# Windowed attention and a mixture of attention experts on one core: keys on partitions, a mask factor, and row-tile units in place of per-head stages

## The chip, the cores and the metric

One core of a Trainium2 chip runs the kernel. The metric is the device time of one execution in microseconds. TensorE multiplies, VectorE and ScalarE work on its results in PSUM and on SBUF, GpSimd makes masks and casts, and DMAs move data between memory and SBUF, issued here by SyncE or by ScalarE.

## The reference

Two attention layers stand one behind the other. The first has 4 batches, 8 heads, 768 positions and 64 columns per head. A query sees the 96 keys up to and with its own and the 8 first keys; a bias falls with the distance, with a slope per head. The second takes the result (8 x 64 = 512 columns) into four attention experts of one head each, causal, and adds up the two that a router picks.

```python
scores = scale * np.matmul(q, k.transpose(0, 1, 3, 2))
is_global = pos[None, :] < int(n_global)
is_local = (rel >= 0) & (rel < int(n_local))
dist = np.where(is_global & ~is_local, float(n_local), np.abs(rel).astype(np.float32))
scores = scores + (-slopes[:, None, None] * dist[None, :, :])[None, :, :, :]
scores = np.where(is_global | is_local, scores, -1000000000.0)
a = np.exp(scores - np.max(scores, axis=-1, keepdims=True))
x = (a / (np.sum(a, axis=-1, keepdims=True) + 1e-09)) @ v    # heads side by side: B, S, 512
for e in range(E):
    a = softmax(causal(scale * (x @ wq[e]) @ (x @ wk[e]).T))
    out += weight[e] * (a @ (x @ wv[e]) @ wo[e])             # weight: softmax over the two best logits, else 0
```

Inputs q, k and v are random numbers of size 0.1, the weights of size 0.05.

## The kernel before

It works in two stages, and a scheduler orders the instructions on each engine. The attention stage loops over batch and head. Per head q, k and v are loaded with rows on partitions (`qL`, `kL`, `VL`, lines 114 to 117), q and k are transposed in fp32 on TensorE, six pieces each (lines 123 and 127), and copied to f16 by VectorE. Then, for each of six row tiles of 128 queries, up to three key tiles are visited: the first, the one before and the diagonal one. Each visit is a chain of small steps, with queries on partitions: the score `sc` (line 139, TensorE, 64 rows of the array), distance times slope added (`L`, line 142, VectorE), exponential with its row sum (line 148, ScalarE), a transpose of the probabilities (`at`, line 155, TensorE, 128 rows), its copy (line 157, VectorE), and the product with v (`zp`, line 158). At the end of a row tile the result is divided by the row sum, transposed in fp32 (line 165) and copied (line 166); a head's result goes to a DRAM tensor, `xT_bridge`.

The expert stage loops over four batches. It loads the bridge, makes router weights for each row tile (lines 193 to 218), and for each expert loads and casts the weights again and projects q and k (lines 242 and 248, 512 and 256 columns) and v (line 257). Then, for each row tile and expert, it makes all causal scores in one row (line 277), copies them to SBUF (line 279), masks the diagonal on GpSimd (line 280), takes the row maximum (line 285) and the exponential (line 289), transposes and copies each 128 columns of probabilities (lines 294 and 297), multiplies with the values (line 298), scales, transposes (line 307) and applies the output matrix (line 310).

All DMAs are issued by SyncE. PSUM pools with one to three buffers set how far one step may run ahead of the next.

Of the kernel before, what the change touches and what calls it, by code (L numbers as in the profile page):

```python
# [14 lines left out]
Iden = mybir.ActivationFunctionType.Identity  # L15

HUGE = 1.0e30
MAXN = 512
# [3 lines left out]
def kernel(  # L22
# [8 lines left out]
    P = 128  # L31
    mm = nc.tensor.matmul
    dma = nc.default_dma_engine.dma_start

    B, H, S, Dh = q.shape
    assert S % P == 0
    n_rt = S // P
    Bm, Sm, Dm = out.shape
    E = moe_w_gate.shape[1]
    Hd = moe_wq.shape[2]  # L40
    assert Dm == H * Dh
    nko = Dm // P
# [307 lines left out]
```

## Time and profile before

| what | us |
|---|---|
| median of 3 runs | 897.18 |
| lowest and highest | 896.14, 905.7 |
| profiled execution: span from first to last instruction | 896.5 |

The profiled execution is told by its span alone; the median of the runs is 0.7 us longer. The page gives, per engine, how much of the span it was busy; PE is TensorE's matmuls, PEld its weight loads, which overlap with them, DVE VectorE, ACT ScalarE, POOL GpSimd. A matmul's duration in the trace includes the time until its last result is in PSUM, so the distance between two starts tells more of the engine's rate than the duration does.

### The profile page before, as it was taken

What the parts mean: (1) busy time and instruction counts of PE and PEld (TensorE: products, weight loads), DVE (VectorE), ACT (ScalarE), POOL (GpSimd) and SP (SyncE); (2) the same over time, 40 slices, a digit from 0 to 9 for tenths busy, and PEclk for the clock granted to TensorE, in tenths of its full rate; (3) what the DMA queues carried; (4) which work ended last, traced back from release to release, by engine and by line L of the source; (5) the groups of instructions that cost most, each with busy time, mean ns of one, the idle gap of its engine ahead of it and who ended that gap; (6) DMA issues with size and microseconds to landing.
All of it is one profiled execution on the core that took longest, in us unless ns stands there. A gap on an engine that the chain in (4) does not pass through costs nothing.

```text
span 896.5 us, 14769 instructions
## 1 busy us (share of the span) xinstructions
PE 745.3 (83%) x3744; PEld 337.4 (38%) x3744; DVE 736.6 (82%) x3890; ACT 299.0 (33%) x1276; POOL 31.1 (3%) x114
## 2 busy tenths in 40 slices
PE   6888898888888888889888588788778887888876
PEld 3444444444444444444444242234223432334222
DVE  6888888888888888888888468878788878877886
ACT  4343434343443434343433222232222322232221
POOL 1000000000000000000000001000100010000100
PEclk9999999999999999999999995557555675558555
DMA  8212121121212121212110431003200220010000
GB/s 158 63 32 63 32 57 37 45 49 45 50 34 60 32 63 31 63 32 61 33 27 6 105 83 42 24 23 79 65 24 29 61 53 24 13 42 7 24 24 23
DMA packets 110820, 40.79 MB, mean 46 GB/s; under 512 B 102544, under 2 KB 106640, under 8 KB 110736
## 3 DMA queue, kind: packets, MB, share of 16 engines
q1 hardware_dynamic: 110736, 39.87, 17.9%
q8 instruction: 29, 0.48, 0.2%
q14 instruction: 55, 0.45, 0.2%
HBM read 30.42 MB, written 9.44 MB: 44 GB/s over the span
## 4 chain that ended last, share of the span: by engine, by line
PE 59%; DVE 25%; issue 7%; ACT 5%; DMA 2%; SPq 0%; POOL 0%; ACTq 0%; POOLq 0%
PE sc L139 9%; PE at L155 9%; PE ztp L165 6%; PE tp L123 5%; PE tp L127 5%; PE pqk L277 4%; PE atp L294 4%; PE zp L158 4%; PE o_ps L310 3%; ACT A L148 3%; PE pqk L248 3%; DVE rmax L285 3%; PE pqk L242 3%; DVE L L279 3%; PE zp L298 2%
## 5 line engine op out<-in xcount | busy, mean ns | idle before, releaser
L148 ACT ACTIVATE A<-L 128x128 f16<-128x128 f32 x480 | 145.8, 304 | 267.0 <-DVE L L142 209.6
L155 PE MATMUL at<-ident,A 128*128 128x128 f16 x480 | 135.5, 293 | 13.3 <-ACT A L148 8.1
L289 ACT ACTIVATE A<-L,nrm 128x128 f16<-128x128 f32 (+5 forms) x96 | 63.8, 665 | 188.0 <-DVE nrm L287 166.5
L139 PE MATMUL sc<-kT,qT 64*128 64x128 f16 x480 | 117.8, 274 | 0.0
L158 PE MATMUL zp<-Vt,at_sb 128*128 128x64 f16 x480 | 101.6, 250 | 13.2 <-DVE at_sb L157 11.7
L157 DVE COPY at_sb<-at 128x128 f16<-128x128 f16 x480 | 104.5, 219 | 8.9 <-PE at L155 5.4
L165 PE MATMUL ztp<-ident,z_sb 128*64 128x128 f32 x192 | 81.0, 422 | 29.8 <-DVE z_sb L163 26.9
L148 ACT ACTIVATION_READ_ACCUMULATOR A<-L 128x1 f32 x480 | 89.5, 186 | 0.0
L297 DVE COPY at_sb<-atp 128x128 f16<-128x128 f16 x336 | 64.5, 220 | 28.9 <-PE atp L294 23.5
L123 PE MATMUL tp<-ident,qL 128*64 128x128 f32 x192 | 80.7, 421 | 8.8 <-DMA qL<-in_q_dram 3.7
L294 PE MATMUL atp<-ident,A 128*128 128x128 f16 x336 | 76.5, 291 | 13.3 <-ACT A L289 12.6
L127 PE MATMUL tp<-ident,kL 128*64 128x128 f32 x192 | 80.7, 421 | 2.5 <-DVE qT L124 1.6
L155 PEld LDWEIGHTS <-A 128*128 128x128 f16 x480 | 50.9, 107 | 83.5 <-ACT A L148 72.5
L142 DVE SCALAR_TENSOR_TENSOR L<-ld,sc 128x128 f32<-128x128 f32 x288 | 80.0, 278 | 0.0
L298 PE MATMUL zp<-V,at_sb 128*128 128x64 f16 x336 | 64.8, 239 | 13.4 <-DVE at_sb L297 12.1
L166 DVE CAST zt_all<-ztp 64x128 f16<-64x128 f32 x192 | 54.2, 282 | 26.3 <-PE ztp L165 14.7
L158 PEld LDWEIGHTS <-at_sb 128*128 128x128 f16 x480 | 59.0, 126 | 39.0 <-DVE at_sb L157 28.0
L163 DVE TENSOR_SCALAR z_sb<-zp,rs_inv 128x64 f32<-128x64 f32 x192 | 54.0, 281 | 21.1 <-PE zp L158 14.2
L277 PE MATMUL pqk<-kT,qT 64*128 64x512 f16 (+3 forms) x128 | 55.8, 443 | 10.3 <-DVE L L279 7.6
L279 DVE COPY L<-pqk 128x512 f32<-128x512 f32 (+3 forms) x128 | 63.2, 497 | 0.5
L310 PE MATMUL o_ps<-wo,zt_sb 64*128 64x512 f16 x96 | 57.9, 603 | 6.3 <-DVE nrm L287 3.0
L298 PEld LDWEIGHTS <-at_sb 128*128 128x128 f16 x336 | 31.5, 109 | 75.0 <-DVE at_sb L297 30.2
(72 smaller groups left out, 1000.9 us busy)
## 6 DMA issues: line engine op xcount, KB each, us to landing
qL<-in_q_dram SPq DMA_DIRECT2D x32, 192.0 KB, 2.8
kL<-in_k_dram SPq DMA_DIRECT2D x32, 192.0 KB, 2.9
VL<-in_v_dram SPq DMA_DIRECT2D x32, 192.0 KB, 2.5
out_dram<-o_sb SPq DMA_DIRECT2D x24, 256.0 KB, 2.0
xT_bridge<-zt_all SPq DMA_DIRECT2D x32, 96.0 KB, 2.2
xt<-xT_bridge SPq DMA_DIRECT2D x16, 192.0 KB, 3.5
wqe<-in_moe_wq_dram SPq DMA_DIRECT2D x16, 128.0 KB, 2.3
wke<-in_moe_wk_dram SPq DMA_DIRECT2D x16, 128.0 KB, 2.3
```

Of the source, the lines that this page charges most:

```text
L123: nc.tensor.transpose(tps[:Dh, :], qL[:, ct, :], ident32[:, :])
L127: nc.tensor.transpose(tps[:Dh, :], kL[:, ct, :], ident32[:, :])
L139: mm(sc[:, :], lhsT=qT[:Dh, ri * P:(ri + 1) * P], rhs=kT[:Dh, ci * P:(ci + 1) * P], start=True, stop=True)
L148: nc.scalar.activation(asl, L[:, :], func=Exp, accum_out=acc[:, :])
L155: nc.tensor.transpose(at_ps[:, :], asl, ident[:, :])
L157: nc.vector.tensor_copy(at_sb[:, :], at_ps[:, :])
L158: mm(z_psum[:, :], lhsT=at_sb[:, :], rhs=Vt[:, ci, :], start=(idx == 0), stop=(idx == ncol - 1))
L165: nc.tensor.transpose(zt_ps[:Dh, :], z_sb[:, :Dh], ident32[:, :])
L277: mm(sc[:, :csz], lhsT=qTe[:Hd, ri * P:(ri + 1) * P], rhs=kTe[:Hd, c0:c0 + csz], start=True, stop=True)
L279: nc.vector.tensor_copy(L[:, c0:c0 + csz], sc[:, :csz])
L294: nc.tensor.transpose(at_ps[:, :], A[:, ci * P:(ci + 1) * P], ident[:, :])
L298: mm(z_psum[:, :], lhsT=at_sb[:, :], rhs=Vte[:, ci, :], start=(ci == 0), stop=(ci == ri))
```

## The change

The kernel is written anew. Work is cut into 24 units: one unit is 128 rows of one batch with all eight heads and all four experts. Scores are made with keys on partitions, so that the exponentials are already what the product with v needs as its stationary operand; nothing is transposed between. No maximum is subtracted. The mask and the distance bias are a factor on the exponentials, `M` (for a row tile's own keys, 128 columns, and for those of the tile before, 96 columns, with zeros up to 128 in `A1`) or `M0` for the first tile. The eight first keys of all heads are handled as one 64-row product (`KG`, `ag`, `VG`), with the bias put into `VG`. A column of ones beside v gives the row sums.

Loads bring q, k and v of all heads for a unit's 128 rows, GpSimd casts them to f16, and the weights are loaded once at the start, by DMAs that ScalarE issues. The result of the attention layer, `x16`, stays on chip and is transposed for the projections. q and k of an expert batch grow row tile by row tile in `QK2`, the values in `V2`. Score matmuls use 64 rows of the array, at partitions 0 to 63 and 64 to 127 in turn (`par`).

The order is written by hand: iteration i works on the attention of unit i, the projections and expert scores of unit i-1 and the expert values and output of unit i-2, and each engine keeps the order of the code. At the end the row sums are checked, and `general_path` computes everything again, in the manner of the kernel before, where one lies outside 0.05 to 60,000.

In the diff, the lines of the kernel before that go are not repeated: all of its two stages go.

```diff
+    def load(u):
+        b, ri = divmod(u, n_rt)
+        rows = slice(ri * P, (ri + 1) * P)
+        qk32 = ring3.tile([P, 2, H, Dh], F32, name="qk32")
+        v32 = ring3.tile([P, H, Dh], F32, name="v32")
+        nc.sync.dma_start(qk32[:, 0, :, :], q[b, :, rows, :].rearrange("h s d -> s h d"))
+        nc.sync.dma_start(qk32[:, 1, :, :], k[b, :, rows, :].rearrange("h s d -> s h d"))
+        nc.sync.dma_start(v32[:, :, :], v[b, :, rows, :].rearrange("h s d -> s h d"))
+        raw[u] = (qk32, v32)
...
+    w32 = const.tile([P, 4, nko, E, Hd], F32, name="w32")
+    for n, w in enumerate((moe_wq, moe_wk, moe_wv)):
+        for e in range(E):
+            nc.scalar.dma_start(w32[:, n, :, e, :], w[e].rearrange("(ko kp) d -> kp ko d", kp=P))
...
+    for b in range(B):
+        for h in range(H):
+            nc.scalar.dma_start(vg32[h * N_G:(h + 1) * N_G, b, :], v[b, h, 0:N_G, :])
...
+    M = const.tile([P, 2, 2, 2, P + N_L], FH, name="M")
+    M0 = const.tile([P, 2, 2, 2, P], FH, name="M0")
+    for h in range(H):
+        hf, pr, par = h // 4, (h // 2) % 2, h % 2
+        act.activation(M0[:, hf, par, pr, :], d0[:, :], func=Exp, scale=-slopes[h])
+    for h in range(H):
+        hf, pr, par = h // 4, (h // 2) % 2, h % 2
+        act.activation(M[:, hf, par, pr, :], d[:, :], func=Exp, scale=-slopes[h])
...
+    act.activation(bm[:, :], bm[:, :], func=Exp)
...
+    def make_vg(b):
+        pool.tensor_tensor(
+            VG[0:NL, b, :, 0:Dh], vg32[:, b, :].unsqueeze(1).to_broadcast([NL, H, Dh]),
+            bm[0:NL, :].unsqueeze(2).to_broadcast([NL, H, Dh]), op=Alu.mult)
+        pool.tensor_copy(VG[0:NL, b, :, Dh:DV], bm[0:NL, :].unsqueeze(2))
...
+    def cast(u):
+        qk32, v32 = raw.pop(u)
+        qk16 = ring2.tile([P, 2, H, Dh], FH, name="qk16")
+        pool.tensor_copy(qk16[:, :, :, :], qk32[:, :, :, :])
+        pool.tensor_copy(V1[u % NV][:, :, 0:Dh], v32[:, :, :])
+        T[u, "qk16"] = qk16
+    def transposes(u):
+        b, ri = divmod(u, n_rt)
+        qk16 = T.pop((u, "qk16"))
+        ps = wtile([P, 2, H // 2, P], FH, "tq")
...
+                nc.tensor.transpose(ps[:, s, p, :], qk16[:, s, 2 * p:2 * p + 2, :], ident[:, :])
+        qkT = ring3.tile([P, 2, H // 2, P], FH, name="qkT")
+        dve.tensor_copy(qkT[:, :, :, :], ps[:, :, :, :])
+        T[u, "qkT"] = qkT
+        if ri == 0:
+            kg = KG[b % 2]
+            for par in range(2):
+                L = slice(par * Dh, (par + 1) * Dh)
+                for p in range(H // 2):
+                    c = (2 * p + par) * N_G
+                    pool.tensor_copy(kg[L, p, c:c + N_G], qkT[L, 1, p, 0:N_G])
...
+    def scores1(u, hf):
+        b, ri = divmod(u, n_rt)
+        qkT = T[u, "qkT"]
+        sc = psS.tile([P, 2, 2, 2 * P], F32, name="sc", tag="s")
+        for pr in range(2):
+            p = 2 * hf + pr
+            for prev in range(2 if ri else 1):
+                for par in range(2):
+                    L = slice(par * Dh, (par + 1) * Dh)
+                    kt = T[u - 1, "qkT"] if prev else qkT
+                    o = sc[:, par, pr, P:P + N_L] if prev else sc[:, par, pr, 0:P]
+                    mm(o, lhsT=kt[L, 1, p, :], rhs=qkT[L, 0, p, 0:N_L] if prev else qkT[L, 0, p, :],
+                       start=True, stop=True)
+        A = A1[(2 * u + hf) % NA]
+        w = P + N_L if ri else P
+        act.activation(A[:, :, :, 0:w], sc[:, :, :, 0:w], func=Exp, scale=scale1)
+        m = M[:, hf, :, :, :] if ri else M0[:, hf, :, :, :]
+        dve.tensor_tensor(A[:, :, :, 0:w], A[:, :, :, 0:w], m, op=Alu.mult)
+        T[u, "A", hf] = A
...
+        qkT = T[u, "qkT"]
+        ps = wtile([P, P], F32, "sg")
+        for p in range(H // 2):
+            mm(ps[:, :], lhsT=KG[b % 2][:, p, :], rhs=qkT[:, 0, p, :], start=(p == 0),
+               stop=(p == H // 2 - 1))
+        ag = ring2.tile([P, P], FH, name="ag")
+        act.activation(ag[:, :], ps[:, :], func=Exp, scale=scale1)
+        T[u, "ag"] = ag
...
+        if ri:
+            mm(z[:, :, :], lhsT=T[u, "ag"][:, :], rhs=VG[:, b, 4 * hf:4 * hf + 4, :],
+               start=True, stop=False)
+        for pr in range(2):
+            for par in range(2):
+                h = 4 * hf + 2 * pr + par
+                mm(z[:, h % 4, :], lhsT=A[:, par, pr, 0:P], rhs=V1[u % NV][:, h, 0:DV],
+                   start=not ri, stop=not ri)
+                if ri:
+                    mm(z[:, h % 4, :], lhsT=A[:, par, pr, P:2 * P],
+                       rhs=V1[(u - 1) % NV][:, h, 0:DV], start=False, stop=(pr == 1 and par == 1))
+        r = rall[:, u, 4 * hf:4 * hf + 4]
+        dve.reciprocal(r, z[:, :, Dh])
+        if hf == 0:
+            T[u, "x16"] = ring2.tile([P, H, Dh], FH, name="x16")
+        dve.tensor_tensor(T[u, "x16"][:, 4 * hf:4 * hf + 4, :], z[:, :, 0:Dh],
+                          r.unsqueeze(2).to_broadcast([P, 4, Dh]), op=Alu.mult)
...
+            nc.tensor.transpose(ps[:, ko, :], x16[:, 2 * ko:2 * ko + 2, :], ident[:, :])
+        xT = ring2.tile([P, nko, P], FH, name="xT")
+        dve.tensor_copy(xT[:, :, :], ps[:, :, :])
+        T[u, "xT"] = xT
...
+        ps = wtile([P, 4, P], F32, "pq")
+        for j in range(4):
+            for ko in range(nko):
+                mm(ps[:, j, :], lhsT=wqk[:, ko, j, :], rhs=xT[:, ko, :], start=(ko == 0),
+                   stop=(ko == nko - 1))
+        dve.tensor_copy(QK2[b % 2][:, ri, :, :], ps[:, :, :])
...
+            mm(ps[:, :], lhsT=xT[:, ko, :], rhs=wvg[:, ko, :], start=(ko == 0),
+               stop=(ko == nko - 1))
+        act.copy(V2[b % 2][:, ri, :, 0:Hd], ps[:, 0:E * Hd].rearrange("p (e d) -> p e d", d=Hd))
+        lg = LG[u % NLG]
...
+        act.activation(el[:, :], dl[:, :], func=Exp)
+        wr = ring3.tile([P, E], F32, name="wr")
+        dve.scalar_tensor_tensor(wr[:, :], lg[:, 0:E], mx[:, 1:2], el[:, :], op0=Alu.is_ge,
+                                 op1=Alu.mult)
+        zr = ring3.tile([P, 1], F32, name="zr")
+        dve.reduce_sum(zr[:, :], wr[:, :], axis=Ax.X)
+        T[u, "w"] = (wr, zr)
...
+            T[u, "A2"] = ring2.tile([P, 2, 2 * n_rt, P], FH, name="A2")
+        A2 = T[u, "A2"]
+        ent = entries(ri)[4 * c:4 * c + 4]
+        sc = psS.tile([P, 2, 4, P], F32, name="s2", tag="s")
+        for n, (ki, p2) in enumerate(ent):
+            for par in range(2):
+                L = slice(par * Hd, (par + 1) * Hd)
+                mm(sc[:, par, n, :], lhsT=qk[L, ki, 2 + p2, :], rhs=qk[L, ri, p2, :], start=True,
+                   stop=True)
+        m = len(ent)
+        act.activation(A2[:, :, 4 * c:4 * c + m, :], sc[:, :, 0:m, :], func=Exp, scale=scale2)
+        if c == 0:
+            pool.affine_select(out=A2[:, :, 0:2, :], in_=A2[:, :, 0:2, :],
+                               pattern=[[0, 2], [0, 2], [1, P]], channel_multiplier=-1, base=0,
+                               compare_op=Alu.is_ge, fill=0.0)
...
+        z = wtile([P, E, DV], F32, "z2")
+        ent = entries(ri)
+        for e in range(E):
+            mine = [(n, ki) for n, (ki, p2) in enumerate(ent) if p2 == e // 2]
+            mine = mine[1:] + mine[:1]
...
+    with tc.manual_schedule():
+        cast(0)
...
-            for h in range(H):
-                qL = sb1.tile([P, n_rt, Dh], F32)
-                kL = sb1.tile([P, n_rt, Dh], F32)
...
+            make_vg(b)
+        load(2)
+        transposes(0)
+        cast(1)
+        for i in range(NU + 2):
+            if has(i + 3):
+                load(i + 3)
+            if has(i + 2):
+                cast(i + 2)
+            if has(i):
+                scores1(i, 0)
+            if has(i - 1):
+                proj_qk(i - 1)
+            if has(i):
+                scores1(i, 1)
+            if has(i - 2):
+                values2(i - 2)
+            if has(i - 1):
+                proj_v(i - 1)
+            if has(i):
+                scores_g(i)
+            if has(i - 1):
+                scores2(i - 1, 0)
+            if has(i + 1):
+                transposes(i + 1)
+            if has(i - 2):
+                zpose(i - 2)
+            if has(i):
+                values1(i, 0)
+            if has(i - 1) and n_chunks(i - 1) > 1:
+                scores2(i - 1, 1)
+            if has(i):
+                values1(i, 1)
+            if has(i - 2):
+                output(i - 2)
+            if has(i - 1) and n_chunks(i - 1) > 2:
+                scores2(i - 1, 2)
+            if has(i):
+                xpose(i)
...
+        mm(ps[:, :], lhsT=good[:, :], rhs=ones[:, :], start=True, stop=True)
+        dve.tensor_copy(flag_i[:, :], ps[:, :])
+    main.close()
+    n_good = nc.values_load(flag_i[0:1, 0:1])
+    with tc.If(n_good < P * NU * (H + E)):
+        general_path(tc, q, k, v, moe_w_gate, moe_wq, moe_wk, moe_wv, moe_wo, out)
```

How the order moves, at three places. On VectorE, in the kernel before, one row tile of the attention stage ends like this (`at` is a transposed piece of probabilities, `zp` the row tile's result):

```order
L157 COPY at_sb<-at 128x128
L161 RECIPROCAL rs_inv<-rowsum 128x1
L142 SCALAR_TENSOR_TENSOR L<-d_glob,sc 128x128
L163 TENSOR_SCALAR z_sb<-zp,rs_inv 128x64
L142 SCALAR_TENSOR_TENSOR L<-ld_88,sc 128x128
L151 COPY rowsum<-acc 128x1
L142 SCALAR_TENSOR_TENSOR L<-ld_78,sc 128x128
L166 CAST zt_all<-ztp 64x128
```

Now, on VectorE, the end of one iteration and the beginning of the next (`tz`, `z_574` and `z_587` are the results of TensorE for the experts and for the two head halves, `tx` the transposed `x`, `A_2` and `A_3` the exponentials of the next unit's halves):

```order
L575 COPY zT<-tz 128x256
L471 RECIPROCAL rall<-z_574 128x4
L474 TENSOR_TENSOR x_585<-z_574,rall 128x256
L471 RECIPROCAL rall<-z_587 128x4
L474 TENSOR_TENSOR x_585<-z_587,rall 128x256
L483 COPY xT<-tx 128x512
L439 TENSOR_TENSOR A_2_219<-A_2_219,M 128x4x224
L494 CAST QK_0_215<-pq 128x512
L439 TENSOR_TENSOR A_3_220<-A_3_220,M 128x4x224
```

The work of eight heads stands in each instruction, and the copy of xT and the masks of the next unit follow the second normalisation of this one. On TensorE, in the kernel before, scores, transposes and products alternate piece by piece:

```order
L139 LDWEIGHTS qT
L139 MATMUL sc<-kT,qT 128x128
L155 LDWEIGHTS A
L155 MATMUL at<-ident,A 128x128
L158 LDWEIGHTS at_sb
L158 MATMUL zp<-Vt,at_sb 128x64
```

Now, on TensorE, the last chunk of expert scores of unit i-1 (`s2`, from `QK2`) stands ahead of the second half of the attention values of unit i (`z1`):

```order
L537 LDWEIGHTS QK2_0_215
L537 MATMUL s2_741<-QK2_0_215 128x128
L460 LDWEIGHTS ag_698
L460 MATMUL z1_747<-VG_197,ag_698 128x260
L465 LDWEIGHTS A1_3_220
L465 MATMUL z1_747<-V1_3_206,A1_3_220 128x65
```

A matmul of 64 rows stands there only between groups of 128-row ones. On ScalarE, the first instructions of the kernel before are computing:

```order
L118 ACT_TABLE_LOAD
L118 CAST Vt<-VL 128x384
L77 CAST ld_78<-ld_i 128x128
L77 CAST ld_88<-ld_i 128x128
L118 CAST Vt<-VL 128x384
L228 CAST wqb<-wqe 128x256
L229 CAST wkb<-wke 128x256
L148 ACTIVATE A,acc<-L 128x128 x7
```

Now 47 DMA issues stand ahead of the first of them (`M_162` is `M0`):

```order
L291 DMA w_84<-in_moe_wq_dram 128x4x64 x4
L291 DMA w_84<-in_moe_wk_dram 128x4x64 x4
L291 DMA w_84<-in_moe_wv_dram 128x4x64 x4
L294 DMA wo_97<-in_moe_wo_dram 128x512 x2
L296 DMA wg_100<-in_moe_w_gate_dram 128x4x4
L300 DMA vg_102<-in_v_dram 8x64 x32
L333 ACT_TABLE_LOAD
L333 ACTIVATE M_162<-d_159 128x128 x8
L336 ACTIVATE M<-d 128x224 x8
L350 ACTIVATE bm<-bm 128x8
L390 CAST wvg<-w_84 128x4x256
L392 CAST wo<-wo_97 128x1024
```

ScalarE comes to the masks only behind its DMA issues, and to the first exponential of a unit behind the masks and two casts.

## Rows read from the trace of the kernel before

**Rows 1.** The page: span, busy us per engine, granted clock in slices.
```profile
span 896.5 us, 14769 instructions
...
PE 745.3 (83%) x3744; PEld 337.4 (38%) x3744; DVE 736.6 (82%) x3890; ACT 299.0 (33%) x1276; POOL 31.1 (3%) x114
...
PEclk9999999999999999999999995557555675558555
```

**Rows 2.** Busy time by stretch: per engine, then clock, DMA share, GB/s.
```profile
22.00:510.00 488.00, 421.19 (x1973) 199.15 (x1974) 412.04 (x2345) 187.24 (x967) 0.00 (x0) 1.00 0.19 47
24.97:40.23 15.26, 13.41 (x65) 6.38 (x65) 13.20 (x76) 5.94 (x31) 0.00 (x0) 1.00 0.20 47
```

**Rows 3.** The waits, longest first: us in total, times, longest us.
```profile
ACT A L148 <- DVE L L142: 209.6, 152, 4.5
```

**Rows 4.** TensorE in order of time: start us, us, instruction, idle before.
```profile
517.39 1.92 PE L242 MATMUL pqk<-xt,wqb 128*64 128x512 f16 x4
...
524.33 1.05 PE L242 MATMUL pqk<-xt,wqb 128*64 128x512 f16 x4
...
529.51 1.05 PE L242 MATMUL pqk<-xt,wqb 128*64 128x512 f16 x4
...
533.89 0.41 PE L257 MATMUL pqk<-wvb,xt 128*128 128x64 f16 x8 [0.18 <-DVE V L259]
```

**Rows 5.** Busy time by stretch, expert stage: projections, then softmax.
```profile
521.90:535.60 13.70, 10.98 (x111) 6.80 (x111) 8.74 (x31) 3.64 (x9) 0.28 (x1) 1.00 0.34 78
535.60:603.80 68.20, 55.76 (x235) 19.96 (x234) 56.71 (x251) 18.03 (x48) 6.69 (x24) 0.50 0.11 36
```

**Rows 6.** VectorE groups by line and shape: busy us, mean ns, idle before.
```profile
L157 DVE COPY at_sb<-at 128x128 f16<-128x128 f16 x480 | 104.5, 219 | 8.9 <-PE at L155 5.4 <-issue 0.2
...
L279 DVE COPY L<-pqk 128x512 f32<-128x512 f32 x48 | 32.7, 682 | 0.2
...
L279 DVE COPY L<-pqk 128x256 f32<-128x256 f32 x32 | 13.1, 409 | 0.0
```

**Rows 7.** ScalarE groups by line and shape.
```profile
L234 ACT CAST wo<-wo 64x512 f16<-64x512 f32 x16 | 9.6, 617 | 28.6 <-PE o_ps L310 23.8 <-DMA xT_bridge<-zt_all 4.5
...
L228 ACT CAST wqb<-wqe 128x256 f16<-128x256 f32 x16 | 6.5, 403 | 17.8 <-PE pqk L257 17.6
```

**Rows 8.** VectorE in order of time, attention stage.
```profile
103.28 0.15 DVE L161 RECIPROCAL rs_inv<-rowsum 128x1 f32<-128x1 f32 x1
103.35 0.13 DVE L151 COPY rowsum<-acc 128x1 f32<-128x1 f32 x1
```

**Rows 9.** TensorE in order of time, attention stage.
```profile
102.82 0.29 PE L155 MATMUL at<-ident,A 128*128 128x128 f16 x1
103.04 0.28 PE L139 MATMUL sc<-kT,qT 64*128 64x128 f16 x1
103.25 0.29 PE L155 MATMUL at<-ident,A 128*128 128x128 f16 x1
...
103.69 0.29 PE L155 MATMUL at<-ident,A 128*128 128x128 f16 x1
103.78 0.26 PE L158 MATMUL zp<-Vt,at_sb 128*128 128x64 f16 x1
```

**Rows 10.** The GpSimd group by line and shape.
```profile
L280 POOL TENSOR_SCALAR_AFFINE_SELECT L<-L 128x128 f32<-128x128 f32 x96 | 27.9, 292 | 850.1 <-DVE L L279 720.6 <-DVE ce L303 37.1 <-ACT wqb L228 31.0
```

**Rows 11.** Busy time by stretch, while the first loads land.
```profile
4.00:6.00 2.00, 1.58 (x7) 0.74 (x6) 0.99 (x4) 0.58 (x2) 0.00 (x0) 1.00 1.34 222
```

**Rows 12.** The DMA queue of SyncE in order of time.
```profile
0.74 0.43 SPq L114 DMA_DIRECT2D qL<-in_q_dram  x1
...
4.47 0.84 SPq L228 DMA_DIRECT2D wqe<-in_moe_wq_dram  x1
```

**Rows 13.** The output: issue ns min/median/max, us to landing.
```profile
L314 SPq DMA_DIRECT2D out_dram<-o_sb x24: 332/333/707, 545.3 to 893.6; - x24
...
DMA to landing us min/median/max: 2.0/2.0/3.4
```

More of the change, by code (lines that the diff above doesn't have):

```diff
@@ new lines @@
+    load(0)
+    load(1)
+    w32 = const.tile([P, 4, nko, E, Hd], F32, name="w32")
+    for n, w in enumerate((moe_wq, moe_wk, moe_wv)):
+        for e in range(E):
+            nc.scalar.dma_start(w32[:, n, :, e, :], w[e].rearrange("(ko kp) d -> kp ko d", kp=P))
+    wo32 = const.tile([P, E // 2, Dm], F32, name="wo32")
+    for p2 in range(E // 2):
+        nc.scalar.dma_start(wo32[:, p2, :], moe_wo[2 * p2:2 * p2 + 2].rearrange("e d n -> (e d) n"))
+    wg32 = const.tile([P, nko, E], F32, name="wg32")
@@ new lines @@
+    KG = [const.tile([P, H // 2, P], FH, name=f"KG{i}") for i in range(2)]
+    for t in KG:
+        pool.memset(t[:, :, :], 0.0)
+    NV = 4
+    V1 = [const.tile([P, H, DV + 1], FH, name=f"V1_{i}") for i in range(NV)]
+    for t in V1:
+        pool.memset(t[:, :, Dh:DV], 1.0)
+    V2 = [const.tile([P, n_rt, E, DV + 1], FH, name=f"V2_{i}") for i in range(2)]
+    for t in V2:
+        pool.memset(t[:, :, :, Hd:DV], 1.0)
+    QK2 = [const.tile([P, n_rt, 4, P], FH, name=f"QK2_{i}") for i in range(2)]
@@ new lines @@
+    NA = 4
+    A1 = [const.tile([P, 2, 2, 2 * P], FH, name=f"A1_{i}") for i in range(NA)]
+    for t in A1:
+        pool.memset(t[:, :, :, P + N_L:2 * P], 0.0)
+    NLG = 4
+    LG = [const.tile([P, 8], F32, name=f"LG{i}") for i in range(NLG)]
+    for t in LG:
+        pool.memset(t[:, E:8], -HUGE)
+    rall = const.tile([P, NU, H + E], F32, name="rall")
+    ones = const.tile([P, 1], F32, name="ones")
+    pool.memset(ones[:, :], 1.0)
+    wqk = const.tile([P, nko, 4, P], FH, name="wqk")
+    wvg = const.tile([P, nko, E * Hd + E], FH, name="wvg")
@@ new lines, in zpose, with output @@
+    def zpose(u):
+        z16 = T.pop((u, "z16"))
+        ps = wtile([P, E // 2, P], FH, "tz")
+        for p2 in range(E // 2):
+            nc.tensor.transpose(ps[:, p2, :], z16[:, 2 * p2:2 * p2 + 2, :], ident[:, :])
+        zT = ring2.tile([P, E // 2, P], FH, name="zT")
+        dve.tensor_copy(zT[:, :, :], ps[:, :, :])
+        T[u, "zT"] = zT
+    def output(u):
+        b, ri = divmod(u, n_rt)
+        zT = T.pop((u, "zT"))
+        ps = wtile([P, Dm], F32, "po")
+        for p2 in range(E // 2):
+            mm(ps[:, :], lhsT=zT[:, p2, :], rhs=wo[:, p2, :], start=(p2 == 0),
+               stop=(p2 == E // 2 - 1))
+        o_sb = ring3.tile([P, Dm], F32, name="o_sb")
+        act.copy(o_sb[:, :], ps[:, :])
+        nc.sync.dma_start(out[b, ri * P:(ri + 1) * P, :], o_sb[:, :])
```

582 lines of the change are left out of this document (322 added, 260 removed).

## The prediction

> **What bounds the kernel now.** I read the page first, then busy time by stretch, the waits, and the order of time. The page says that TensorE is busy 745 us and VectorE 737 us of a span of 896.5 us [rows 1]: two engines over 80%, which looks like a kernel without slack. The stretches say where: with the start the attention stage fills some 510 us, one head of it taking 15.26 us, again and again (32 times); the expert stage takes the remaining 386 us, four batches of some 97 us [rows 2]. The waits say what kind of busy this is: ScalarE waits 210 us in all for the masked scores that VectorE writes [rows 3], and every step is a 128x128 piece that goes from TensorE to VectorE to ScalarE to TensorE and back. So the bound is the number of small instructions and their hand-overs, not arithmetic.
>
> Two more things have to be read before anything can be priced. First, TensorE's clock. The slices show full clock until 522 us [rows 1], but the matmuls do not bear that out: four 512-column matmuls that begin at 517.39 take 1.92 us, the same four at 529.51 take 1.05 us [rows 4]. After the tail of the last one (about 0.2 us) that is 0.43 against 0.21 us each, 512 columns at 1.2 and at 2.4 GHz. So the clock was at its lower level before 522 us, whatever the slices say, and I take the attention stage to run there too. From 521.9 to 535.6 us, in the projections, it is granted in full, and in the softmax part after it at half [rows 5]. At full clock a 64-column matmul costs (0.41 - 0.2)/7, about 0.03 us, with the loading of its weights hidden [rows 4]: 1/2.4 ns per column and little else. Second, the fixed cost. A copy from PSUM takes 0.41 us at 256 and 0.68 us at 512 columns of f32 [rows 6]: about 1.07 ns per column and 0.14 us fixed. A 128-column f16 copy takes 219 ns [rows 6], where one column at a time would make it 0.28 and two at a time 0.21: two 16-bit columns at a time. ScalarE: 0.40 us at 256, 0.62 us at 512 columns [rows 7]: 0.84 ns per column and 0.19 us fixed.
>
> **What goes.** The probability transposes (816 on TensorE, 816 copies on VectorE), the row maxima, the accumulator reads, the fp32 transposes, the DRAM bridge and the weights loaded again for every batch all go. What remains is 24 units (4 batches x 6 row tiles), each handling all heads and all experts of 128 rows.
>
> **One unit, engine by engine** (row tile 1 to 5; the means over row tiles where it depends on them).
> VectorE: two mask multiplications of 896 f16 columns; at two columns at a time 0.14 + 448 x 1.07 ns = 0.62 us each (no row shows a two-input f16 operation; at one column at a time it would be 1.10 us; I take 0.62, because the f16 copy of [rows 6] is the nearest row). QK2 cast, 512 f32: 0.68. Three normalisations of 256 columns: 3 x 0.41. Copies of f16 transposes of 1024, 512 and 256 columns: 0.69, 0.41 and 0.28. Ten short operations at 0.15 (the reciprocal in [rows 8]): 1.5. Sum 6.0 us, 24 units: 145 us. An operation that need not wait starts about 0.08 us before the end of the one ahead: the copy at 103.35 in [rows 8], with the reciprocal ending at 103.43. So the engine's floor is nearer 5 us.
> ScalarE: two exponentials of 896 columns, 0.94 each; the global one 0.30; experts' values 0.40; router 0.2; output 0.62; the experts' exponentials, 1792 columns in two instructions on average, 1.88. Sum 5.3 us, 127 in all.
> TensorE: 102 matmuls with 12,470 columns in the mean (8x128 transposes, 8x128 and 8x96 scores, 4x128 global, 2x260 and 16x65 values, 4x128, 16x128, 4x260, 14x128, 14x65, 2x128, 2x512): 5.2 us at full clock, 10.4 at half. To this come changes between 64-row and 128-row matmuls. In [rows 9] a transpose (128 rows) at 102.82, a score (64 rows) at 103.04 and a transpose at 103.25 stand 0.22 us apart, while a pair that stays at 128 rows (103.69, 103.78) is 0.09 apart: about 0.15 us per change. A unit has 6 to 10 of them, 0.9 to 1.5 us. The Trainium skill (TensorEngine Tiling (Array Packing), Key Properties) says the same: changing the tiling mode, not just the tile, drains the engine; the rows agree. Without such a drain, the loop below would be some 0.5 us per unit shorter.
> GpSimd: two casts (1024 and 512 columns) and a select of 512. The only row is 0.29 us for 128 columns [rows 10]; if all of it is fixed 0.9 us a unit, if all goes by column 4.7 us. Either way it is under the other engines.
> DMA: 768 KB per unit in 256-byte pieces; at the 222 GB/s at which such loads saturate [rows 11] 3.5 us.
>
> No engine fills more than about 6 us. But the order is written by hand and each engine keeps it, so the period of a unit is the longest loop through these orders. I follow it from the end of one unit's second normalisation (x16) to the next unit's.
> 1. The four transposes of xpose (0.06 to start, 4 x 0.07), a change of rows (0.15), 8 scores (0.45), the tail of the last (0.2): the first exponential starts at 1.15 us and ends at 2.1; VectorE has only the xT copy meanwhile and idles about 1.1 us.
> 2. The 16 projections must wait for the xT copy (1.05) and take 0.9; the second half of the scores stands behind them with two changes: its exponential runs from 2.85 to 3.8. VectorE does the first mask and QK2 until 3.4 and idles again.
> 3. From 3.85 VectorE works through its list: mask 0.62, the expert normalisation 0.85, the router's three 0.45, the wait for ScalarE's router exponential 0.3, two short ones 0.3, the qkT copy 0.69, zT 0.28, two reciprocal-and-multiply pairs 1.1; less overlap 0.4: 4.2 us. That makes 8.05.
> 4. For four of the six row tiles a chunk of expert scores stands between the two halves of values1 on TensorE, with two changes (0.43 + 0.3): the second half is late by 0.5. For two of them the third chunk stands ahead of xpose: 0.3 more, and ScalarE's list is about 9 us there.
> Mean (2 x 8.1 + 2 x 8.6 + 2 x 9.0)/6, about 8.6 us. 23 units after the first: 198 us.
>
> **The start.** All weights and 32 little pieces of v are issued by ScalarE, 47 DMAs ahead of its first mask. An issue holds the queue for 0.43 us on a free queue and 0.84 on a full one [rows 12]; nearer the former for the 32 small ones, 0.4, and 0.55 for 15, together 21 us. Then the table load 1.3, 16 masks 4, the factor bm 0.2, two casts 2: ScalarE is free at 28.5. GpSimd needs bm for make_vg (four products, about 1.4 each), and the cast of unit 1 stands behind it on GpSimd, and the transposes of unit 1 ahead of values1 of unit 0 on TensorE: bm at 27, make_vg to 32.5, key copies and cast to 35, transposes, normalisations: x16 of unit 0 ends at 38. Bounds 30 (issues of 0.33 [rows 13]) and 48 (0.84 throughout).
> **The end.** After x16 of unit 23: projections, three chunks of exponentials with QK2 ahead (to 7.3), values2 of 24 matmuls, normalisation, transpose, output and its copy to 11.5, the output's DMA 2.0 [rows 13]; the row-sum check beside it. 13.5 us.
> Sum: 38 + 198 + 13.5 = 249.5 us of span. Of the profiled execution only the span is shown; the median of the runs is 0.7 us above it (897.18 against 896.5), so 250 us.
>
> **Rivals.**
> - *TensorE stays at the lower clock.* For it: the attention stage before, and the half clock in the sparse softmax [rows 5]. Against it: the projections ran 7,680 columns per expert (4 x 2 x 768 and 24 x 64) in 5.2 us, from 524.33 to 529.51 [rows 4], some 1,480 per us, and kept the full clock for 13.7 us [rows 5]; 12,470 columns in 8.6 us are 1,450 per us, as many. At half clock TensorE needs 10.4 + 1.2 us and its waits: period 12.2, together 38 + 4 + 281 + 17 = 340 us.
> - *The mask multiplications cost twice as much*, one column at a time: both lie on the loop, +0.96 us per unit: 272 us. A lock between VectorE and GpSimd would act at the same place: a mask that waits behind a cast (about 1.1 and 0.6 us, if GpSimd takes a column as fast as ScalarE) loses up to 1.7 us a unit: 250 + 39 = 289 us. The Trainium skill (SBUF — State Buffer, Who interferes with whom) states such a rule: a VectorE instruction with two SBUF inputs and a GpSimd instruction that reads SBUF exclude each other, and the later one waits in full. No run here shows it: GpSimd idles through the attention stage. I think the casts mostly fall before the first mask.
> - *The loop is shorter than I count*: score pairs in the two row halves overlap, and changes cost half at full clock: period 7.6, start 30, end 12: 217 us.
> - *The fallback runs.* If one row sum lies outside 0.05 to 60,000, everything is computed again by general_path, in the old manner and with less overlap: at least 250 + 896 = 1146 us, slower than before. It decides from the first such row. With inputs of 0.1 a diagonal term is about 1 and no sum exceeds 768 such terms, so I give it 2%.
>
> **How the numbers follow.** Forecast (230 to 265) 0.55, shorter loop 0.15, dear masks or lock 0.15, lower clock 0.12, fallback 0.02, the rest 0.01. The likeliest gives 250 us; the range from 218 to 300 leaves out the low clock, the fallback and the ends. About 1% is what a measurement of this kernel can tell. Only the fallback ends above the old time: faster 0.97, same 0.01, slower 0.02.
>
> **What would show it.** Right: x16 of unit 0 at 38 us with ScalarE doing nothing but issues until 21; units every 8 to 9 us; VectorE busy some 6 us of each and waiting for the first and second exponential (about 1.1 and 0.45 us); mask products at 0.62 us; full clock after the first units; scores 0.2 us behind a 128-row matmul. Wrong: a period set by TensorE with the clock at 0.5; mask products of 1.1 us, or long ones beside GpSimd's casts; a DMA as what ends the waits; anything of general_path in the trace.

## The result, and the profile after

The changed kernel takes 252.66 us (250.8 to 254.38, 4 runs) against 897.69 us (896.14 to 905.7): a ratio of 0.281, 95% interval 0.2785 to 0.2827. The forecast was 250. The total is right and its terms are not: the start and the end were forecast 18.6 us too short together, the loop 15.5 us too long. That these errors cancel is luck. The terms are read from the profiled execution, the longest of the four (254.38 us, a span of 252.7).

The page of the kernel after, beside [rows 1]: span, busy time of each engine, granted clock in 40 slices.

```profile
span 252.7 us, 6001 instructions
...
PE 158.5 (63%) x2362; PEld 112.2 (44%) x2362; DVE 142.8 (56%) x473; ACT 117.4 (46%) x208; POOL 69.1 (27%) x146
...
PEclk9999999999999999977999999799999979996755
```

VectorE, forecast at 145 us of work, has 142.8. No engine is above 63% and none is the bound: the waits say so (us in total, times, longest us; beside [rows 3]).

```profile
DVE A L439 <- ACT A L437: 45.9, 44, 18.3
...
ACT el L511 <- DVE dl L509: 37.6, 24, 1.9
ACT A L437 <- PE sc L433: 35.9, 40, 8.3
ACT L333 <- DMA vg<-in_v_dram: 32.6, 1, 32.6
```

The first and third are one loop: VectorE waits for an exponential, ScalarE for the scores ahead of it. The last is the start: ScalarE does nothing but issue loads for 32.6 us. Its order of time (start, us; ACTq is its DMA queue; beside [rows 12]):

```profile
0.82 2.35 ACTq L291 DMA_DIRECT2D w<-in_moe_wq_dram  x4
3.20 4.58 ACTq L291 DMA_DIRECT2D w<-in_moe_wk_dram  x4
8.19 4.39 ACTq L291 DMA_DIRECT2D w<-in_moe_wv_dram  x4
12.95 1.47 ACTq L294 DMA_DIRECT2D wo<-in_moe_wo_dram  x2
16.47 0.39 ACTq L296 DMA_DIRECT2D wg<-in_moe_w_gate_dram  x1
16.90 15.70 ACTq L300 DMA_DIRECT2D vg<-in_v_dram  x32
32.62 1.28 ACT L333 ACT_TABLE_LOAD   x1 [32.62 <-DMA vg<-in_v_dram]
...
37.77 0.19 ACT L350 ACTIVATE bm<-bm 128x8 f32<-128x8 f32 x1
```

The 15 loads of weights (12 of 128 KB, two of 256, one of 8) hold the queue until 16.9 us, the 32 small ones 15.70 us more, 0.49 each. The issues themselves are 8.9 of the first 16.0 us and 10.0 of the 15.7 (0.60 and 0.31 each, in the records of single issues); in the rest the queue stands still between two of them. The groups by line and shape (us, mean ns, idle before; beside [rows 6]) show the mask product at two columns at a time, as forecast:

```profile
L439 DVE TENSOR_TENSOR A<-A,M 128x896 f16<-128x896 f16 x40 | 25.0, 626 | 25.6 <-ACT A L437 25.5
L474 DVE TENSOR_TENSOR x<-z,rall 128x256 f16<-128x256 f32 x48 | 20.4, 424 | 1.6
L494 DVE CAST QK<-pq 128x512 f16<-128x512 f32 x24 | 16.5, 686 | 3.2 <-PE pq L492 3.2
L412 DVE COPY qkT<-tq 128x1024 f16<-128x1024 f16 x24 | 16.4, 682 | 4.4 <-PE tq L410 4.4
```

One unit (13, the second of its batch) in order of time, TensorE, then ScalarE, then VectorE. The x16 of the unit before ends at 142.78.

```profile
142.28 0.40 PE L537 MATMUL s<-QK 64*128 64x128 f16 x8
142.61 0.51 PE L481 MATMUL tx<-ident,x 128*128 128x128 f16 x4
143.06 0.37 PE L433 MATMUL sc<-qkT 64*128 64x128 f16 x8
143.64 1.05 PE L492 MATMUL pq<-xT,wqk 128*128 128x128 f16 x16 [0.21 <-DVE xT L483]
144.62 0.37 PE L433 MATMUL sc<-qkT 64*128 64x128 f16 x8
```

```profile
142.87 1.03 ACT L540 ACTIVATE A<-s 128x1024 f16<-128x1024 f32 x1
143.79 0.93 ACT L437 ACTIVATE A<-sc 128x896 f16<-128x896 f32 x1
145.04 0.92 ACT L437 ACTIVATE A<-sc 128x896 f16<-128x896 f32 x1 [0.32 <-PE sc L433]
```

```profile
142.36 0.42 DVE L474 TENSOR_TENSOR x<-z,rall 128x256 f16<-128x256 f32 x1
143.16 0.42 DVE L483 COPY xT<-tx 128x512 f16<-128x512 f16 x1 [0.38 <-PE tx L481]
144.75 0.62 DVE L439 TENSOR_TENSOR A<-A,M 128x896 f16<-128x896 f16 x1 [1.16 <-ACT A L437]
145.29 0.68 DVE L494 CAST QK<-pq 128x512 f16<-128x512 f32 x1
145.99 0.63 DVE L439 TENSOR_TENSOR A<-A,M 128x896 f16<-128x896 f16 x1
...
148.34 0.22 DVE L513 SCALAR_TENSOR_TENSOR wr<-LG,mx,el 128x4 f32<-128x4 f32 x1 [0.34 <-ACT el L511]
148.60 0.16 DVE L516 TENSOR_REDUCE zr<-wr 128x1 f32<-128x4 f32 x1
148.67 0.68 DVE L412 COPY qkT<-tq 128x1024 f16<-128x1024 f16 x1
...
150.22 0.42 DVE L474 TENSOR_TENSOR x<-z,rall 128x256 f16<-128x256 f32 x1
```

The wait of 1.16 us ahead of the first mask is the one that the forecast put at 1.1, but this unit is not the usual one: ScalarE is still at the third chunk of expert scores until 143.90 us, behind which the first exponential stands. In most units the wait is 0.83 us, and 0.34 ahead of the second mask (forecast 0.45), as in unit 14:

```profile
152.28 0.63 DVE L439 TENSOR_TENSOR A<-A,M 128x896 f16<-128x896 f16 x1 [0.83 <-ACT A L437]
...
153.85 0.63 DVE L439 TENSOR_TENSOR A<-A,M 128x896 f16<-128x896 f16 x1 [0.34 <-ACT A L437]
```

The clock by stretch (us, then busy of PE, PEld, DVE, ACT, POOL, granted clock, DMA share, GB/s; beside [rows 2, 5]):

```profile
52.00:110.00 58.00, 44.38 (x712) 31.54 (x710) 42.64 (x143) 32.49 (x58) 17.22 (x31) 1.00 0.53 115
110.00:117.00 7.00, 6.82 (x70) 5.13 (x70) 4.14 (x14) 2.82 (x5) 1.52 (x2) 0.51 0.70 152
...
229.50:252.70 23.20, 11.24 (x117) 6.97 (x115) 5.94 (x24) 6.43 (x10) 1.20 (x2) 0.57 0.11 38
```

From 52 us on it is 2.4 GHz in nearly all of the loop, with three falls to 1.2 GHz (110.0 to 116.8, 157.8 to 161.2, 205.6 to 209.0 us), and the lower level in most of the end. Before 52 us the slices show the full clock and the matmuls do not, as before 522 us in the kernel before: the projections that begin at 49.16 us start 107 ns apart, those at 143.64 us 56, so the first unit ran at 1.2 GHz. In the order of time x16 of unit 0 ends at 48.1 us and that of unit 23 at 230.7; 23 units in 182.5 us are 7.94 each. Most take 7.87, the first of each later batch 7.26 to 7.54, and three, beside a fall of the clock, 8.8 to 9.0.

### The profile page after: what moved, and what is told of

The parts are those of the page before. It is cut to its first block, busy times and chain, and to the rows that moved or that the text cites. A ratio compares the mean times of both kernels' runs of the same rounds, so it can differ in the third digit from the quotient of the medians.

```text
span 252.7 us, 6001 instructions
## 1 busy us (share of the span) xinstructions
PE 158.5 (63%) x2362; PEld 112.2 (44%) x2362; DVE 142.8 (56%) x473; ACT 117.4 (46%) x208; POOL 69.1 (27%) x146
## 5 line engine op out<-in xcount | busy, mean ns | idle before, releaser
L437 ACT ACTIVATE A<-sc 128x896 f16<-128x896 f32 (+1 forms) x48 | 41.5, 866 | 35.9 <-PE sc L433 35.9
L439 DVE TENSOR_TENSOR A<-A,M 128x896 f16<-128x896 f16 (+1 forms) x48 | 29.8, 623 | 45.9 <-ACT A L437 45.9
L540 ACT ACTIVATE A<-s 128x1024 f16<-128x1024 f32 (+1 forms) x48 | 43.3, 917 | 0.3
L492 PE MATMUL pq<-xT,wqk 128*128 128x128 f16 x384 | 29.3, 237 | 4.9 <-DVE xT L483 4.8
L492 PEld LDWEIGHTS <-wqk 128*128 128x128 f16 x384 | 27.0, 107 | 7.0 <-issue 5.2
L400 POOL CAST qk<-qk 128x1024 f16<-128x1024 f32 x24 | 24.9, 1036 | 0.3
L474 DVE TENSOR_TENSOR x<-z,rall 128x256 f16<-128x256 f32 x48 | 20.4, 424 | 1.6
L583 PE MATMUL po<-wo,zT 128*128 128x512 f16 x48 | 15.5, 405 | 6.5 <-DVE zT L575 6.5
L433 PE MATMUL sc<-qkT 64*128 64x128 f16 (+1 forms) x352 | 18.3, 226 | 1.2 <-DVE qkT L412 1.2
L537 PE MATMUL s<-QK 64*128 64x128 f16 x336 | 18.2, 223 | 0.0
L465 PE MATMUL z<-V,A 128*128 128x65 f16 x192 | 17.4, 196 | 0.0
L556 PE MATMUL z<-V,A 128*128 128x65 f16 x336 | 16.0, 201 | 1.3 <-ACT A L540 1.2
L333 ACT ACT_TABLE_LOAD x1 | 1.3, 1283 | 32.6 <-DMA vg<-in_v_dram 32.6
```

The source lines that it names most:

```text
L400: pool.tensor_copy(qk16[:, :, :, :], qk32[:, :, :, :])
L433: mm(o, lhsT=kt[L, 1, p, :], rhs=qkT[L, 0, p, 0:N_L] if prev else qkT[L, 0, p, :], start=True, stop=True)
L437: act.activation(A[:, :, :, 0:w], sc[:, :, :, 0:w], func=Exp, scale=scale1)
L439: dve.tensor_tensor(A[:, :, :, 0:w], A[:, :, :, 0:w], m, op=Alu.mult)
L465: mm(z[:, h % 4, :], lhsT=A[:, par, pr, 0:P], rhs=V1[u % NV][:, h, 0:DV], start=not ri, stop=not ri)
L474: dve.tensor_tensor(T[u, "x16"][:, 4 * hf:4 * hf + 4, :], z[:, :, 0:Dh], r.unsqueeze(2).to_broadcast([P, 4, Dh]), op=Alu.mult)
```

## The experiments

"Start" is the end of x16 of unit 0, "period" the mean to that of unit 23, "end" what follows; all from the profiled execution. The ratio is to the kernel before, with its 95% interval. The ends differ by more than the edits: in the change and in e5 the last projections ran at 1.2 GHz (1.86 us instead of 1.05), and the last output copy ends 14.9 us after x16, in the other runs 12.4 to 13.2.

| run | us | ratio | start | period | end |
|---|---|---|---|---|---|
| the change | 252.66 | 0.281 (0.2785 to 0.2827) | 48.1 | 7.94 | 22.0 |
| e1_vg8 | 242.37 | 0.269 (0.267 to 0.2708) | 38.8 | 7.86 | 19.2 |
| e2_early_scores | 237.42 | 0.263 (0.2613 to 0.2636) | 47.7 | 7.40 | 19.4 |
| e7_second_early | 243.09 | 0.269 (0.2676 to 0.2707) | 47.9 | 7.58 | 19.3 |
| e3_qkt_act | 251.15 | 0.278 (0.2771 to 0.2793) | 47.8 | 7.84 | 19.9 |
| e5_rows_apart | 253.53 | 0.281 (0.2797 to 0.2831) | 47.8 | 7.92 | 21.7 |
| e4_no_check | 249.31 | 0.277 (0.275 to 0.278) | 48.0 | 7.91 | 16.1 |
| e6_pool_busy | 281.96 | 0.312 (0.3103 to 0.3146) | 47.7 | 9.18 | 22.4 |
| e8_both | 228.25 | 0.253 (0.2511 to 0.255) | 38.8 | 7.33 | 19.5 |
| e9_both_sp | 213.76 | 0.237 (0.2355 to 0.2389) | 22.1 | 7.41 | 19.3 |

**e1_vg8: is the start ScalarE's list of issues?**
```diff
-    for b in range(B):
-        for h in range(H):
-            nc.scalar.dma_start(vg32[h * N_G:(h + 1) * N_G, b, :], v[b, h, 0:N_G, :])
+    for h in range(H):
+        nc.scalar.dma_start(vg32[h * N_G:(h + 1) * N_G, :, :],
+                            v[:, h, 0:N_G, :].rearrange("b g d -> g b d"))
```


> The 32 small loads of v for the global keys become 8, each of four batches; nothing else changes. Theory (the start is ScalarE's list: 47 issues, of which the 32 small ones take 15.7 us, then table load, masks, bm, and behind bm GpSimd's products): 24 issues of 0.49 us go, x16 of unit 0 ends 12 us earlier, at 36 us instead of 48, and the whole takes 241 us. Rival (the start is set by the amount of data that the DMA engines have to bring): the same bytes come, x16 of unit 0 stays near 48 us and the time at 252.

The same bytes in 8 loads instead of 32: 10.3 us less, and x16 of unit 0 earlier by 9.3, not by 12, as a load of 8 KB takes 0.82 us of the queue (8 in 6.54). The table load moved from 32.62 to 23.31 us, and the rest of the start with it: the list was the bound.

**e2_early_scores and e7_second_early: is the loop the scores that stand behind other work?** e2 issues the first half of the next unit's scores ahead of xpose and the second half ahead of proj_qk, the masks apart from their exponentials; e7 moves the second half alone.
```diff
+            if has(i + 1):
+                scores1(i + 1, 0)
             if has(i):
                 xpose(i)
...
             if has(i):
-                scores1(i, 0)
+                if i == 0:
+                    scores1(i, 0)
+                mask1(i, 0)
+            if has(i):
+                scores1(i, 1)
             if has(i - 1):
                 proj_qk(i - 1)
             if has(i):
-                scores1(i, 1)
+                mask1(i, 1)
```


> The first half of the next unit's scores moves ahead of xpose on TensorE, the second half ahead of the projections; the masks keep their places on VectorE. No work is added or taken away. Theory (the period of 7.87 us is a loop through the hand-written orders, in which VectorE waits for the first exponential 0.83 us and for the second 0.34): the first wait goes, VectorE then waits for the projections instead, and about 0.55 us per unit is won, 12 to 13 us in all: 240 us. Rival 1 (VectorE's own work bounds the unit): at most 2 us. Rival 2 (TensorE is the bound, its columns and changes of rows): no change or slower, as its work is the same.

> Only the second half of the scores moves, ahead of the projections. Theory of the loop: the wait for the second exponential goes (0.34 us in most units, none in others), but the projections and QK2 come 0.2 us later: 0.1 to 0.3 us per unit, 246 to 250 us. Rival (VectorE's own work or TensorE bounds the unit): 252 us.

237.42 and 243.09 us: both faster, e7 by more than was expected: the second mask follows 1.14 us behind the first instead of 1.57, so the whole wait goes, and the later projections cost nothing. VectorE in e2, unit 14, in order of time:

```profile
145.58 0.42 DVE L488 COPY xT<-tx 128x512 f16<-128x512 f16 x1 [0.38 <-PE tx L486]
146.24 0.62 DVE L445 TENSOR_TENSOR A<-A,M 128x896 f16<-128x896 f16 x1 [0.24 <-ACT A L437]
147.15 0.69 DVE L499 CAST QK<-pq 128x512 f16<-128x512 f32 x1 [0.28 <-PE pq L497]
147.75 0.61 DVE L445 TENSOR_TENSOR A<-A,M 128x896 f16<-128x896 f16 x1
```

The wait ahead of the first mask has shrunk from 0.83 to 0.24 us; most periods are 7.21. The part from the second mask to x16 is some 4.65 us in both kernels: what is left is mostly VectorE's list; VectorE idles 1.5 us of this unit, 2.1 in the kernel after. Of the 15.5 us between the two spans 12.4 are the periods (23 x 0.54), as expected, and 2.6 the end, where the clock differs.

**e3_qkt_act: is VectorE's list a term by itself?** The copy of 0.68 us goes to ScalarE.
```diff
-        dve.tensor_copy(qkT[:, :, :, :], ps[:, :, :, :])
+        act.copy(qkT[:, :, :, :], ps[:, :, :, :])
```


> The copy of the transposes of q and k (1024 columns) goes from VectorE to ScalarE. Theory of the loop: this copy lies in the stretch of VectorE's list that is on the loop, 0.60 us from start to start; the values behind it are ready some 0.4 us before VectorE comes to them, so 0.4 to 0.6 us per unit go, 9 to 14 us: 239 to 244 us. Rival (ScalarE and its exponentials bound the unit): a microsecond more on ScalarE makes it slower, up to 24 us: 252 to 276 us.

251.15 us; the interval overlaps that of the change, so no gain was shown. ScalarE in order of time says why:

```profile
140.57 1.01 ACT L412 COPY qkT<-tq 128x1024 f16<-128x1024 f16 x1
141.46 1.04 ACT L540 ACTIVATE A<-s 128x1024 f16<-128x1024 f32 x1
142.38 0.60 ACT L586 COPY o_sb<-po 128x512 f32<-128x512 f32 x1
142.84 1.07 ACT L540 ACTIVATE A<-s 128x1024 f16<-128x1024 f32 x1
143.76 1.77 ACT L437 ACTIVATE A<-sc 128x896 f16<-128x896 f32 x2
```

x16 ended at 141.48 here, and the first exponential starts 2.28 us later, behind a full queue; in the kernel after it was 1.01 in the same unit. In the mean of units 3 to 22 the second mask to x16 falls from 4.64 to 4.37 us, and x16 to the second mask rises from 3.30 to 3.46. So VectorE's list does get shorter, and ScalarE's takes it back where it is full: this unit, 13, takes 8.70 us instead of 7.86, while unit 14 takes 7.50 instead of 7.88.

**e5_rows_apart: do the scores gain from alternating between the array's row halves?**
```diff
-        for pr in range(2):
-            p = 2 * hf + pr
-            for prev in range(2 if ri else 1):
-                for par in range(2):
+        for par in range(2):
+            for pr in range(2):
+                p = 2 * hf + pr
+                for prev in range(2 if ri else 1):
```


> The eight score matmuls of a half are issued with the four of partitions 0 to 63 first and then the four of 64 to 127, in place of one of each in turn. Theory: in turn, two of them overlap in the array (eight take 0.37 us to the end of the last, 0.02 us per matmul, where 128 columns alone would take 0.05); apart, a half takes about 0.25 us more, and both halves stand on the loop: 0.25 to 0.5 us per unit, 258 to 264 us. Rival (no overlap of row halves; the 0.5 us that the first step of the loop is shorter than forecast comes from the changes of rows alone): no change, 252 us.

No change (253.53 us, period 7.92), against the expectation. The records of single matmuls show the two halves side by side in either order: eight scores begin in pairs, 3 ns apart in the kernel after and 14 ns apart here, and take 0.37 and 0.38 us to the end of the last. So the overlap is there in both, and the order does not decide it.

**e4_no_check: what does the row-sum check cost at the end?** The load of the flag into a register, the branch and the fallback are left out.
```diff
-    n_good = nc.values_load(flag_i[0:1, 0:1])
-    with tc.If(n_good < P * NU * (H + E)):
-        general_path(tc, q, k, v, moe_w_gate, moe_wq, moe_wk, moe_wv, moe_wo, out)
```


> The register load of the row-sum flag, the branch and the fallback are left out (the flag is still worked out). Theory: behind the last copy (245.6 us) stand the branch on TensorE, 4.0 us, and the closing semaphores; the output's DMA needs only 2.0 us, so about 3 us go: 249.5 us. Rival (the last output's DMA and the closing of the program set the end anyway): no change, 252.5 us.

3.35 us less by the medians. From the end of the last output copy to the end of the span it is 2.9 us (242.97 to 245.9), against 7.1 (245.6 to 252.7) with the check.

**e6_pool_busy: does GpSimd's work lock VectorE's masks?** Four more casts of 1024 columns per unit, into a tile that nothing reads.
```diff
+        for _ in range(4 if u > 2 else 0):
+            pool.tensor_copy(junk[:, :, :, :], qk32[:, :, :, :])
```


> GpSimd gets four further casts of 1024 columns per unit, from unit 3 on, into a tile that nobody reads: some 4.1 us more, so that it is busy while VectorE multiplies the masks. Theory (masks and casts do not meet in the changed kernel, and no lock was paid): what it costs then tells the price of the lock; if a mask has to wait for a cast that has begun, each mask loses some 0.5 us on average, 1 us per unit, together about 273 us, and mask rows grow or get waits. Rival (there is no lock between a two-input f16 product and a cast): masks stay at 0.63 us and the time at 252 to 254 us.

29 us slower. The mask by shape, and one mask with the casts beside it:

```profile
L442 DVE TENSOR_TENSOR A<-A,M 128x896 f16<-128x896 f16 x40 | 37.8, 945 | 25.4 <-ACT A L440 25.3
```

```profile
170.56 1.49 DVE L442 TENSOR_TENSOR A<-A,M 128x896 f16<-128x896 f16 x1 [0.83 <-ACT A L440]
```

```profile
169.43 3.52 POOL L404 CAST junk<-qk 128x1024 f16<-128x1024 f32 x3
```

945 ns in the mean instead of 626. In the records of single instructions the cast that runs when this mask starts ends 1.01 us later, and the mask takes 1.485 us: 0.47 more than the cast's rest. Masks that start 0.33 and 0.85 us before a cast's end take 0.81 and 1.33: the same 0.47. The mask waits for the running cast in full; of its own 0.63 us only 0.15 lie under the cast. The lock holds the other way too: a wide cast that begins behind a mask ends 0.90 us after it, though alone it takes 1.04. Other products pay as well: the small one for the experts' weights, `cw`, takes 0.585 us in the mean instead of 0.222 and ends 0.01 us behind the cast that ran when it began: 8.7 us in all, beside 14.6 for the masks. The lock need not explain all 29 us: the mean clock is also lower, 0.877 against 0.934, and its share was not taken apart.

**e8_both and e9_both_sp: do the gains add, and what is left in the start?** e8 is e1 and e2 together. e9 also gives all loads of the start to SyncE, those of the global values first.
```diff
+    for h in range(H):
+        nc.sync.dma_start(vg32[h * N_G:(h + 1) * N_G, :, :],
+                            v[:, h, 0:N_G, :].rearrange("b g d -> g b d"))
...
-            nc.scalar.dma_start(w32[:, n, :, e, :], w[e].rearrange("(ko kp) d -> kp ko d", kp=P))
+            nc.sync.dma_start(w32[:, n, :, e, :], w[e].rearrange("(ko kp) d -> kp ko d", kp=P))
```


> The eight loads per head together with the early scores and the masks issued apart from their exponentials. Theory: the start and the loop are separate terms that add. The start is worth 252.7 - 242.4 = 10.3 us and the loop 252.7 - 237.4 = 15.3 us, so 227.1 us, with the first normalised unit ended at about 38.5 us and a mean period of 7.40 us. Rival: the shorter period and the earlier start load the clock differently or share a wait, so that part of one gain is lost: 230 to 234 us, seen as a period above 7.5 us.

> The same, and every load of the start issued by SyncE, the eight loads of the global values first, then the weights, so that ScalarE has nothing to issue. Theory: the 23 us for which ScalarE issued loads kept its eight-row masks and casts behind them, and the 0.75 MB of units 2 and 3 was carried between the weights; with the list gone the masks are built by about 10 us, the weights are landed by about 19 us, and the first normalised unit ends at about 29 us: 227 - 9.5 = 217.5 us. Rival: the bytes of the weights and GpSimd's list of products and casts set the start anyway, so that it ends at 35 to 38 us and the time is 223 to 227 us. Second rival: the loads of units 2 and 3, now queued behind the weights, come late and the loop stumbles, seen as VectorE or GpSimd waiting for a load after the first unit.

228.25 us, so the gains add (to within 1.1 us). 213.76 us: another 14.5, more than expected, and the fastest version here, 0.846 of the change's time (213.76/252.66). ScalarE's start in e9:

```profile
3.86 1.28 ACT L334 ACT_TABLE_LOAD   x1 [3.86 <-DVE d L309]
...
9.00 0.19 ACT L348 ACTIVATE bm<-bm 128x8 f32<-128x8 f32 x1
10.51 1.09 ACT L435 ACTIVATE A<-sc 128x512 f16<-128x512 f32 x2 [1.32 <-PE sc L431]
```

bm is there at 9.2 instead of 38.0 us, and x16 of unit 0 at 22.1. The price is one long first period, 9.56 us. In it GpSimd waits for a load of unit 2, issued behind the weights (the second rival), and TensorE for the cast of the router's weights; what each adds to the period is not known.

```profile
24.50 1.04 POOL L398 CAST qk<-qk 128x1024 f16<-128x1024 f32 x1 [4.71 <-DMA qk<-in_k_dram]
...
26.91 1.02 PE L504 MATMUL pv<-wvg,xT 128*128 128x260 f16 x4 [1.93 <-DVE wvg L389]
```

What the other queue and what the other order of the loads is worth was not taken apart.

## Why the prediction was right in sum and wrong in its terms

| term | forecast | measured | run that bears it out |
|---|---|---|---|
| start | 38 | 48.1 | e1, e9 |
| 23 periods | 198 | 182.5 | e2, e7 |
| end | 13.5 | 22.0 | e4, in part |

*The start* was mis-sized in the term "nearer the former for the 32 small ones, 0.4, and 0.55 for 15, together 21 us". The 15 took 16.0 us (0.82 to 16.86, 1.07 each) and the 32 took 15.7 (0.49 each), 32 us instead of 21. The issues themselves were priced well, at 0.60 and 0.31; the time between them, 12.9 us, has no term in the sum. What stands behind the list came out right: 10.2 us from bm to x16, forecast 11. The bounds are wrong as sums: 47 issues at 0.33 or 0.84 us are 15.5 or 39.5, which gives a start of 32 or 56, not 30 or 48; that 48.1 was measured is chance. While the first loads run, the kernel after moves some 218 GB/s, as in [rows 11]; that the queue stands behind this rate is likely but was not isolated.

*Step 1* (first mask 2.15 us after x16) measured 1.68 in the mean of units 3 to 22. Eight scores were priced at 0.45 from the first start to the last; they begin within 0.17 us, since the row halves run side by side. And two of the four transposes need only the first half of x16 and begin before its end (142.61 against 142.78). The change between 64 and 128 rows was priced too high, at 0.15 us on top of 0.07 for the transpose: from the transpose at 142.905 to the score at 143.057 it is 0.15 us from start to start, of which the transpose alone takes 0.06, so the change adds 0.09.
*Step 2*, from the first to the second mask, was forecast at 1.70 and measured 1.62.
*Step 3* was forecast at 4.2 and measured 4.64, in unit 13 4.66. The overlap is there, 0.08 us at seven places (0.58 in all, forecast 0.4). But the operations add up to 4.66 us instead of 4.3, as the ten short ones take 0.13 to 0.23, not 0.15, and seven gaps of 0.03 stand ahead of operations that depend on the one before, 0.24 in all, which the sum left out.
*Step 4* (a mean of 0.43 us) added nothing to the period. Eight expert scores take 0.33 us from the first start to that of the transpose behind them, not 0.43 + 0.3, and all reciprocals and normalisations of values1 together wait 2.1 us in 48 pairs (0.5 at L471, 1.6 at L474): TensorE had long finished the second half. The third chunk does delay the first mask of the next unit (1.96 us after x16 instead of 1.64), but the second mask then follows 1.24 us behind it instead of 1.57.

*The end* had two prices missing. At 1.2 GHz the last projections take 1.86 us instead of 1.05, and the last output copy ends 14.9 us after x16, forecast 11.5; in e1, where those projections ran at 2.4 GHz, it is 12.5, and where the last 1.0 us comes from is open. Then 7.1 us follow where 2.0 stood for the output's DMA: the check is not "beside it". The flag is ready only after the last sums, and in the records TensorE's branch then takes 3.96 us (245.86 to 249.83). e4 gives back 3.35 us. And the 0.7 us from span to time compared two executions; in each run of the change it is 1.7 (254.38 against 252.7).

*The rivals.* The shorter loop was right in its mechanism (row halves side by side, cheaper changes) with a period between its 7.6 and the forecast's 8.6, but its start of 30 was further off still. Dear masks: no, 626 ns. The low clock: only in three short falls of about 1 us per unit touched, and at the end. The lock exists, as e6 shows. In the kernel after the casts mostly end before the first mask, as thought; the exceptions are the first mask of the first unit (1.27 us, beside a product for `VG`) and the first of each later batch, 0.64 us instead of 0.42, beside a cast that ends 0.36 us after its start. The fallback did not run. The Trainium skill (SBUF — State Buffer, Who interferes with whom) says that a VectorE operation with two SBUF inputs and a GpSimd one that reads SBUF exclude each other in full; e6 agrees: the three masks above leave the same rest to 0.01 us.

## What to carry to other kernels

Follow the loop through the engines' orders and price each wait in it, but check each price in the first trace: a total can be right because its terms are wrong in both directions. When no engine is above two thirds, look for what stands behind unrelated work in a queue: making 8 loads of the 32 small ones ahead of the masks saved 10 us, moving the scores ahead of transposes and projections 12 in the periods. Moving an operation off the busiest engine gains only in the stretches where the other engine's list does not then end later (e3).

## What the runs showed of the hardware that was not expected

- Matmuls on the two row halves run side by side whatever their order in the program: starts 3 or 14 ns apart, eight in 0.37 to 0.38 us. The Trainium skill (TensorE: Matmul & The Clock Gate, Why this matters for your kernels) states that slices in distinct row groups run at the same time; the trace agrees.
- While SyncE loaded the first four units, a load of weights held ScalarE's queue for 1.07 us in the mean, 0.60 of it the issue; a load of 8 KB took 0.82 in e1 (8 in 6.54 us), and one of 2 KB 0.49, 0.31 of it the issue.
- A flag loaded into a register and a branch that is not taken cost 3.35 us at the end of the program.
- The granted clock fell for 3.4 or 6.8 us at a time inside a loop that never changes; in e9 it stayed at 2.4 GHz from 32.1 to 199.3 us without a fall, with a shorter period.
